# Exponentials left in PSUM, five PSUM banks given out by the list schedule, and late transposes moved to DMA, in an RWKV attention with a multiplicative FFN

## The chip, the cores and the metric

The kernel runs on one core of a Trainium2 chip. The metric is the device time of one launch in microseconds. Smaller is better.

## The reference

```python
B, H, S, D = 4, 8, 768, 48                       # r, k, v, w: [B, H, S, D], u: [H, D], all float32
state = zeros(B, H, D, D)
for t in range(S):
    kt, vt, rt, wt = k[:, :, t], v[:, :, t], r[:, :, t], w[:, :, t]
    cur = einsum('bhd,bhe->bhde', u * kt, vt)
    y[:, :, t] = einsum('bhd,bhde->bhe', rt, state + cur)
    state = wt[..., None] * state + einsum('bhd,bhe->bhde', kt, vt)

x = y.transpose(0, 2, 1, 3).reshape(B * S, H * D)     # 3072 tokens x 384
out = ((x @ w1) * (x @ w2)) @ w3 @ w_out              # 384 -> 1024 -> 1024 -> 384
```

## The kernel before

**Tiling.** The 3072 tokens are cut into 24 chunks of 128 tokens, six for each of the four sequences. A chunk holds all eight heads, so a row of a chunk is 8 x 48 = 384 numbers. The FFN works on blocks of two or four chunks (2, 2, 4, 4, 4, 4, 4).

**The attention of one chunk n**, with the names that its steps have in the code and in the profile:

- The loads `ld_w`, `ld_k`, `ld_r`, `ld_v` bring w, k, r and v of the chunk from DRAM, 192 KB each. SP issues them; there are eight buffers of each kind. k and r lie side by side in one tile, `kr_in`.
- `ln` (ACT) takes the logarithm of w. `cs` (PE, two matmuls) sums it over the tokens with triangular matrices. `ex` (ACT) takes the exponentials, which before go from PSUM to the tile `e_sb` in SBUF. `krt` (DVE) multiplies k and r by them and writes bf16.
- `tr` (PE, eight 128x128 transposes) and `trs` (ACT, copy from PSUM) turn the scaled k and r so that the head dimension lies on the partitions.
- `m` (PE) makes the scores, and `mb` (DVE, tile `mbf`) masks them. `kv` (PE) makes the chunk's contribution to the state and, in an extra column, the chunk's total decay in logarithm. `pc` (ACT) takes its exponential.
- `ts` (DVE) forms the running state, before with four fused multiply-adds; `sbd` (POOL) multiplies it by the decay into a block-diagonal bf16 tile, in two instructions.
- `uk1`, `uk2` (POOL, tile `uk`), `ds` (DVE) and `yd` (POOL) make the u term. `vb` turns v into bf16 (tile `v_bf`).
- `y` (PE) sums the masked scores times v and r times the state of the chunk before; `yb` (DVE, tile `y_bf`) adds the u term. `yt` (PE, three transposes) and `xt` (ACT) turn the result for the FFN, into `xT`.

**The FFN.** For each block and each of eight slices of 128 hidden columns, `a` and `b` (PE, three matmuls each) are formed, `a` is copied to SBUF by ACT (`a_sb`) and DVE multiplies the two (`abT`). w3 and w_out are multiplied once, on the chip: `wt`, `wtc`, `wm`, `wc` make `w34`. `o` (PE, eight matmuls for 128 tokens), a copy by ACT (`o_sb`) and a store issued by SP end it.

**The order of the work.** Nothing is executed in the order in which it is written down. Every step above is given to the class `Plan` with its engine, a planned length, the steps that it needs, the buffers that it takes and frees. `Plan` runs a list schedule: at each turn the step that can start first is placed, and of steps that can start at the same time the one with the lowest rank. The planned times of loads come from a model of the DMA ring with at most eight transfers in flight. The steps are then emitted in the order found, each engine works through its own list in that order, and semaphores enforce the data. So the order on every engine, SP's queue included, is fixed at build time by planned times, and a step that comes later than planned holds everything behind it on its engine. All instructions are emitted through one helper, so that nearly all of them carry one line number.

**The weights** are loaded by DMAs that POOL issues, and that turn float32 into bf16. Each of the seven pieces waits for a POOL step named in `TUNE["triggers"]`.

**PSUM** has eight banks. Before, three belong to the FFN (`f`), two to `tr`, `kv` and `yt` in turn, a pair to `cs` and `m`, and one to `y`.

Of the kernel before, what the change touches and what calls it, by code (L numbers as in the profile page):

```python
# [16 lines left out]
    early=2,  # L17
    triggers=["uk10", "uk21", "uk12", "uk22", "uk22", "uk13", "uk23"],
    lead=5, every=3.9,
    m_one=True, s_dve=False, v_act=2, nudge={},  # L20
# [3 lines left out]
class Plan:  # L24
# [6 lines left out]

    HOP = 0.06
# [7 lines left out]
    def add(self, name, eng, length, fn, needs=(), take=(), free=(), lag=0.03, rank=None, rows=0, big=0):  # L40
        assert name not in self.steps, name
        self.steps[name] = dict(eng=eng, length=length, fn=fn, needs=list(needs), take=list(take),
                                free=list(free), lag=lag,
                                rank=(rank if rank is not None else len(self.steps)) + TUNE["nudge"].get(name, 0),
                                rows=rows, big=big)

    def _pass(self, windows):
        end, eng_free, taken, owner, released = {}, {}, {}, {}, {}
        left = dict(self.steps)
# [12 lines left out]
        while left:  # L62
            best = {}
            for n in ready:
# [14 lines left out]
                if not ok:  # L79
                    continue  # L80
                if s["rows"] and len(ring) >= 8:
                    t = max(t, ring[-8])
                best.setdefault(s["eng"], []).append((t, s["rank"], n))
# [9 lines left out]
            start[n] = t  # L93
            eng_free[s["eng"]] = t + s["length"]
# [25 lines left out]
            for u in users.get(n, ()):  # L120
                waiting[u] -= 1
                if waiting[u] == 0:
                    ready.add(u)
        return order, new_windows, start, end

# [27 lines left out]
def kernel(  # L153
# [49 lines left out]
    ps_t = ctx.enter_context(tc.tile_pool(name="ps_t", bufs=2, space=bass.MemoryType.PSUM))  # L203
    ps_m = ctx.enter_context(tc.tile_pool(name="ps_m", bufs=1, space=bass.MemoryType.PSUM))
    ps_y = ctx.enter_context(tc.tile_pool(name="ps_y", bufs=1, space=bass.MemoryType.PSUM))
# [4 lines left out]
    mask = consts.tile([C, HP, C], BF)  # L210
# [16 lines left out]
                       base=0, channel_multiplier=-1, pattern=[[0, HP], [1, C]])  # L227
# [14 lines left out]
    for i in range(NS):  # L242
# [4 lines left out]
    plan.buffers(w_in=NIN, kr_in=NIN, v_in=NIN, lw=NS, krt=NS, sbd=NS, v_bf=3, e_sb=2, uk=2, ds=2, yd=3,  # L247
                 trs=2, mbf=2, pc=3, ts=3, y_bf=2, a_sb=3, o_sb=3, xT=3, abT=3, w3T=2, f=3, t=2, m=1, y=1)
    T = {}
    EV = -50  # L250
# [34 lines left out]
    def att(n):  # L285
        b, c = divmod(n, NC)
        last = c == NC - 1
        v_act = n >= TUNE["v_act"]
# [5 lines left out]
        def cs():  # L294
            t = T["cs", n] = ps_m.tile([C, 2, TB], F32, tag="m", name="cs")
            for j, lt in enumerate((LTn_incl, LT_strict)):
                pe.matmul(t[:, j, 0:DM], lhsT=lt, rhs=T["lw", n][:, :, 0:D], start=True, stop=True)

        def ex():
            t = T["e", n] = work.tile([C, 2, H, D], F32, tag="e_sb", name="e_sb")  # L300
            act.activation(t.rearrange("t j h d -> t j (h d)"), T["cs", n][:, :, 0:DM], Act.Exp)

        def krt():
            T["krt", n] = kr_st[n % NS]
            dve.tensor_mul(T["krt", n][:, :, :, 0:D], T["kr_in", n], T["e", n])
# [13 lines left out]
        def ds():  # L319
            t = T["ds", n] = work.tile([C, H], F32, tag="ds", name="ds")  # L320
            dve.reduce_sum(t, T["uk", n], axis=mybir.AxisListType.X)
# [5 lines left out]
        def tr():  # L327
            t = T["tr", n] = ps_t.tile([C, 2, HP, C], BF, tag="t", name="tr")
# [5 lines left out]
        def trs():  # L334
            t = T["trs", n] = work.tile([C, 2, HP, C], BF, tag="trs", name="trs")
            act.copy(t, T["tr", n])

        def kv():
            t = T["kv", n] = ps_t.tile([C, HP, D + 1], F32, tag="t", name="kv")
# [9 lines left out]
        def pc():  # L349
            t = T["pc", n] = work.tile([C, HP], F32, tag="pc", name="pc", bufs=3)  # L350
            act.activation(t[:, :, None], T["kv", n][:, :, D:D + 1], Act.Exp)

        def ts():
            t = T["ts", n] = work.tile([C, HP, D], F32, tag="ts", name="ts_", bufs=3)
            if c == 0:
                dve.tensor_copy(t, T["kv", n][:, :, 0:D])
            else:
                for p in range(HP):
                    dve.scalar_tensor_tensor(t[:, p, :], T["ts", n - 1][:, p, :], T["pc", n - 1][:, p:p + 1],
                                             T["kv", n][:, p, 0:D], op0=Alu.mult, op1=Alu.add)  # L360

        def sbd():
            t = T["sbd", n] = sb_st[(b * (NC - 1) + c) % NS]
            for q in range(2):
                o = q * DP
                (dve if TUNE["s_dve"] else pool).tensor_mul(
                    t[o:o + DP, :, q * D:(q + 1) * D], T["ts", n][o:o + DP],
                    T["pc", n][o:o + DP, :, None].to_broadcast([DP, HP, D]))

        def m():  # L370
            t = T["m", n] = ps_m.tile([C, 2, HP, C], F32, tag="m", name="m")
# [7 lines left out]
        def mb(q):  # L379
            if q == 0:  # L380
                T["mb", n] = work.tile([C, 2, HP, C], BF, tag="mbf", name="mbf")
            if TUNE["m_one"]:
                dve.tensor_mul(T["mb", n].rearrange("s q h t -> s (q h) t"),
                               T["m", n].rearrange("s q h t -> s (q h) t"),
                               mask[:, 0:1, :].to_broadcast([C, H, C]))
            else:
                dve.tensor_mul(T["mb", n][:, q], T["m", n][:, q], mask)

        def y():
            t = T["y", n] = ps_y.tile([C, H, D], F32, tag="y", name="y")  # L390
            first = True
            if c > 0:
                for p in range(HP):
                    pe.matmul(t[:, 2 * p:2 * p + 2, :], lhsT=T["trs", n][:, 1, p, :],
                              rhs=T["sbd", n - 1][:, p, :], start=first, stop=False)
# [7 lines left out]
        def yb():  # L403
            t = T["yb", n] = work.tile([C, DM], BF, tag="y_bf", name="y_bf")
            dve.tensor_add(t.rearrange("t (h e) -> t h e", h=H), T["y", n], T["yd", n])

        def yt():
            t = T["yt", n] = ps_t.tile([C, DI, C], BF, tag="t", name="yt")
# [6 lines left out]
        def xt():  # L415
            if n == lo:
                T["xT", j] = big.tile([P, DI, TB], BF, tag="xT", name="xT")
            act.copy(T["xT", j][:, :, (n - lo) * C:(n - lo + 1) * C], T["yt", n])

        A = plan.add  # L420
        A(f"ln{n}", "ACT", 0.46, ln, needs=[f"ld_w{n}"], take=["lw"], free=[f"ld_w{n}"])
        A(f"cs{n}", "PE", 0.33, cs, needs=[f"ln{n}"], take=["m"], lag=0.2, free=[] if not last else [f"ln{n}"])
        A(f"ex{n}", "ACT", 0.75, ex, needs=[f"cs{n}"], take=["e_sb"], free=[f"cs{n}"])
        A(f"krt{n}", "DVE", 1.12, krt, needs=[f"ex{n}", f"ld_k{n}", f"ld_r{n}"], take=["krt"],
          free=[f"ex{n}", f"ld_k{n}"])
        A(f"tr{n}", "PE", 0.46, tr, needs=[f"krt{n}"], take=["t"], lag=0.2, free=[] if not last else [f"krt{n}"])
        A(f"trs{n}", "ACT", 0.95, trs, needs=[f"tr{n}"], take=["trs"], free=[f"tr{n}"])
        A(f"vb{n}", *(("ACT", 0.43) if v_act else ("POOL", 0.55)), vb, needs=[f"ld_v{n}"], take=["v_bf"], free=[f"ld_v{n}"])
        if not last:
            A(f"kv{n}", "PE", 0.42, kv, needs=[f"krt{n}", f"vb{n}"], take=["t"], lag=0.2,  # L430
              free=[f"krt{n}", f"ln{n}"])
            old = [f"ts{n - 1}", f"pc{n - 1}"] if c else []
            A(f"ts{n}", "DVE", 0.48 if c else 0.32, ts, needs=[f"kv{n}"] + old, take=["ts"], free=[f"kv{n}"] + old)
            A(f"pc{n}", "ACT", 0.14, pc, needs=[f"kv{n}"], take=["pc"], free=[f"kv{n}"])
            A(f"sbd{n}", *(("DVE", 0.55) if TUNE["s_dve"] else ("POOL", 1.25)), sbd, needs=[f"ts{n}", f"pc{n}"],
              take=["sbd"], free=[f"ts{n}", f"pc{n}"])
        A(f"m{n}", "PE", 0.36, m, needs=[f"trs{n}"], take=["m"], lag=0.2)
        if TUNE["m_one"]:
            A(f"mb0{n}", "DVE", 1.17, lambda: mb(0), needs=[f"m{n}"], take=["mbf"], free=[f"m{n}"])
        else:  # L440
            A(f"mb0{n}", "DVE", 0.63, lambda: mb(0), needs=[f"m{n}"], take=["mbf"], free=[f"m{n}"])
            A(f"mb1{n}", "DVE", 0.63, lambda: mb(1), needs=[f"mb0{n}"], free=[f"m{n}"])
        A(f"uk1{n}", "POOL", 1.06, uk1, needs=[f"ld_k{n}", "ld_u"], take=["uk"])
        A(f"uk2{n}", "POOL", 1.06, uk2, needs=[f"uk1{n}", f"ld_r{n}"], free=[f"ld_k{n}"])
        A(f"ds{n}", "DVE", 0.5, ds, needs=[f"uk2{n}"], take=["ds"], free=[f"uk1{n}"])
        A(f"yd{n}", "POOL", 0.85, yd, needs=[f"ds{n}", f"vb{n}"], take=["yd"], free=[f"ds{n}"])
        A(f"y{n}", "PE", 0.42, y, needs=[f"mb0{n}" if TUNE["m_one"] else f"mb1{n}", f"vb{n}"] + ([f"sbd{n - 1}"] if c else []), take=["y"], lag=0.2,
          free=[f"mb0{n}", f"trs{n}", f"vb{n}"] + ([f"sbd{n - 1}"] if c else []))
        A(f"yb{n}", "DVE", 0.5, yb, needs=[f"y{n}", f"yd{n}"], take=["y_bf"], free=[f"y{n}", f"yd{n}"])
# [161 lines left out]
```

## Time and profile before

| | |
|---|---|
| median of 8 runs | 193.96 us (192.83 to 195.13) |
| the profiled execution | 195.13 us, of which the span is 193.4 us |
| TensorE clock granted | 1.0 |
| busy: PE, DVE, ACT, POOL | 166.2, 129.2, 116.9, 106.0 us |
| moved by DMA | 28.54 MB, mean 148 GB/s |

The profile is one execution. Its page gives busy time by engine, the span in 40 slices of 4.8 us with the busy share of each in tenths, the chain of work that ended last, and groups of instructions. A group's line reads: engine, operation, output and input tiles with partitions x elements, count, busy time and mean of one in ns, and the engine's idle time before them with what ended most of it. In a list of waits the numbers are the sum in us, how many, and the longest. In the list of instructions in order of time they are start, length, engine, operation, tiles and count; several alike are merged into one entry. PE's busy time counts the latency of pipelined matmuls, so it is more than what the matmuls need when they stream.

### The profile page before, as it was taken

Reading aid. Unit: us, or ns where it says so; the run is one execution under the profiler, and the core shown is the slowest. Engines: PE = TensorE matmul, PEld = TensorE weight load, DVE = VectorE, ACT = ScalarE, POOL = GpSimd, SP = SyncE. Lnnn points to the kernel's source line nnn. Section 1 sums busy time; section 2 is a strip of 40 time slices with the busy share of each in tenths; the row PEclk is TensorE's granted clock in tenths of the full one; section 3 lists DMA queues with packets and bytes.
Section 4 is the critical chain, followed back from the end, with each engine's and each line's share of the span. In section 5 each row is a group of like instructions: output and inputs, shape, how many; then the busy total and the mean of one; then the engine's idle time right before and its main releaser. Section 6 shows DMA issues by size and latency. Waiting matters only on the chain.

```text
span 193.4 us, 4437 instructions
## 1 busy us (share of the span) xinstructions
PE 166.2 (86%) x1658; PEld 103.7 (54%) x1672; DVE 129.2 (67%) x238; ACT 116.9 (60%) x227; POOL 106.0 (55%) x133
## 2 busy tenths in 40 slices
PE   0437896979999989999899999999699999999992
PEld 0214675856776655545565464666355664454450
DVE  6256768554697779897686999797688745422510
ACT  3426455631787777877867976975776834434431
POOL 5498897220496898977795968969623200000000
PEclk9999999999999999999999999999999999999999
DMA  6999999999799899999999989999200021013012
GB/s 117 200 178 171 204 215 190 203 201 185 131 190 191 169 226 195 224 159 192 189 169 235 220 180 187 161 198 218 103 2 3 37 90 41 0 41 124 3 52 111
DMA packets 107159, 28.54 MB, mean 148 GB/s; under 512 B 100353, under 2 KB 106113, under 8 KB 107137
## 3 DMA queue, kind: packets, MB, share of 16 engines
q1 hardware_dynamic: 103440, 23.80, 64.7%
q0 software_dynamic: 3696, 4.46, 13.6%
q8 instruction: 13, 0.21, 0.6%
q14 instruction: 10, 0.07, 0.1%
HBM read 27.98 MB, written 4.72 MB: 169 GB/s over the span
## 4 chain that ended last, share of the span: by engine, by line
PE 44%; DMA 17%; POOL 16%; DVE 8%; ACT 6%; issue 5%; SPq 2%; POOLq 0%; ACTq 0%; DVEq 0%
PE o_ps L148 11%; POOL uk L148 8%; PE b L148 7%; PE a L148 7%; DMA w_bf<-in_moe_w_dram 7%; DMA kr_in<-in_k_dram 6%; PE wm L148 6%; POOL sbd L148 4%; POOL yd L148 4%; ACT e_sb L148 3%; PE tr L148 3%; DVE krt L148 2%; DMA out_dram<-o_sb 2%; DVE mbf L148 2%; PE kv L148 2%
## 5 line engine op out<-in xcount | busy, mean ns | idle before, releaser
L148 PEld LDWEIGHTS <-w_bf 128*128 128x128 bf16 x400 | 35.4, 98 | 27.5 <-issue 2.2
L148 DVE TENSOR_TENSOR abT<-a_sb,b 128x512 bf16<-128x512 f32 (+1 forms) x56 | 33.9, 606 | 22.6 <-PE b L148 12.4
L148 PE MATMUL b<-xT,w_bf 128*128 128x512 bf16 (+1 forms) x161 | 39.9, 350 | 1.0 <-ACT a_sb L148 0.5
L148 PE MATMUL a<-xT,w_bf 128*128 128x512 bf16 (+1 forms) x161 | 39.6, 349 | 1.1 <-ACT xT L148 0.6
L148 ACT COPY a_sb<-a 128x512 f32<-128x512 f32 (+1 forms) x56 | 29.4, 528 | 17.7 <-PE a L148 15.6
L148 PE MATMUL o_ps<-w,abT 128*128 128x384 bf16 x192 | 34.2, 326 | 0.0
L148 POOL TENSOR_TENSOR yd<-v_bf,ds 128x384 bf16<-128x384 bf16 x24 | 25.3, 1054 | 12.8 <-ACT v_bf L148 9.9
L148 DVE TENSOR_TENSOR krt<-kr_in,e_sb 128x768 bf16<-128x768 f32 x24 | 25.6, 1068 | 10.0 <-ACT e_sb L148 9.9
L148 DVE TENSOR_TENSOR mbf<-m,mask 128x1024 bf16<-128x1024 f32 x24 | 29.1, 1214 | 1.5 <-PE m L148 1.5
L148 POOL TENSOR_TENSOR uk<-uk,kr_in 128x384 f32<-128x384 f32 x24 | 25.7, 1073 | 7.3 <-DMA kr_in<-in_r_dram 6.1
L148 POOL TENSOR_TENSOR uk<-kr_in,u_bc 128x384 f32<-128x384 f32 x24 | 25.5, 1064 | 7.6 <-DMA kr_in<-in_k_dram 4.7
L148 ACT COPY trs<-tr 128x1024 bf16<-128x1024 bf16 x24 | 24.4, 1016 | 5.7 <-PE tr L148 5.2
L148 PEld LDWEIGHTS <-krt 128*128 128x128 bf16 (+1 forms) x352 | 17.5, 109 | 15.1 <-DVE krt L148 8.1
L148 PEld LDWEIGHTS <-abT 128*128 128x128 bf16 x192 | 17.8, 98 | 11.6
L148 ACT ACTIVATE e_sb<-cs 128x768 f32<-128x768 f32 x24 | 19.6, 817 | 5.6 <-PE cs L148 5.5
L148 PE MATMUL tr<-I,krt 128*128 128x128 bf16 x192 | 16.0, 231 | 5.0 <-DVE krt L148 5.0
L148 ACT COPY o_sb<-o_ps 128x384 f32<-128x384 f32 x24 | 11.5, 478 | 14.5 <-PE o_ps L148 11.1
L148 ACT ACTIVATE lw<-w_in 128x384 bf16<-128x384 f32 x24 | 12.5, 526 | 7.0 <-DMA w_in<-in_w_dram 7.0
L148 DVE TENSOR_REDUCE ds<-uk 128x8 f32<-128x384 f32 x24 | 13.1, 545 | 5.3 <-POOL uk L148 4.8
L148 DVE TENSOR_TENSOR y_bf<-y,yd 128x384 bf16<-128x384 f32 x24 | 13.2, 550 | 4.5 <-issue 1.9
L148 PEld LDWEIGHTS <-trs 48*128 48x128 bf16 (+1 forms) x272 | 11.6, 99 | 8.3 <-issue 3.0
L148 PE MATMUL cs<-lw,LTn_incl 128*128 128x384 bf16 x24 | 8.4, 351 | 7.2 <-ACT lw L148 5.0
(80 smaller groups left out, 183.5 us busy)
## 6 DMA issues: line engine op xcount, KB each, us to landing
w_in<-in_w_dram SPq DMA_DIRECT2D x24, 192.0 KB, 4.6
kr_in<-in_k_dram SPq DMA_DIRECT2D x24, 192.0 KB, 4.6
kr_in<-in_r_dram SPq DMA_DIRECT2D x24, 192.0 KB, 4.7
v_in<-in_v_dram SPq DMA_DIRECT2D x24, 192.0 KB, 4.6
out_dram<-o_sb SPq DMA_DIRECT2D x24, 192.0 KB, 2.0
w_bf<-in_moe_w_dram POOLq DMA_DIRECT2D x2, 1024.0 KB, 15.5
w_bf<-in_moe_w_dram POOLq DMA_DIRECT2D x4, 384.0 KB, 6.7
wo_bf<-in_moe_w_out_dram POOLq DMA_DIRECT2D x1, 768.0 KB, 11.3
```

Of the source, the lines that this page charges most:

```text
L148: return self.tc.keep_in_program_order(f(*a, **k))
```

## The change

- `ex` writes the exponentials back over the sums in PSUM, and `krt` reads them there; the tile `e_sb` is gone. `pc` does the same with the decay column of `kv`.
- The five banks outside the FFN become three tiles, `g01`, `g23` and `g4`. `cs` and `m` take one of two pairs, and `tr`, `kv`, `y` and `yt` take one of five banks. `Plan` chooses at its turn the bank that comes free first by its planned times; the bank is held until the steps named in `free` are done.
- For chunks 12 to 23, `tr` is dropped and `trs` is a DMA that transposes the scaled k and r from SBUF to SBUF (128 x 1024, bf16). For chunks 16 to 23, `yt` is dropped and `xt` is such a DMA of 128 x 384. SP issues both.
- The state: `ts` adds the chunk's contribution to the decayed state, `st` multiplies by the decay (one DVE instruction each), and `sb` copies it into the block-diagonal tile (POOL, two instructions).
- The mask has one 128 x 128 block; `trs` and `y_bf` get three buffers; SP's steps of non-negative rank may be planned no earlier than 1.5 us before the modelled DMA ring is free.
- Planned lengths, ranks and settings change: which POOL step lets each weight piece go, how many FFN blocks come before `w34` in rank (`early`), and how far the attention's ranks run ahead (`lead`, `every`). `s_act`, `d_pool` at NEVER leave `sb` on POOL and `ds` on DVE.

```diff
 TUNE = dict(
     blocks=[2, 2, 4, 4, 4, 4, 4],
-    early=2,
-    triggers=["uk10", "uk21", "uk12", "uk22", "uk22", "uk13", "uk23"],
-    lead=5, every=3.9,
-    m_one=True, s_dve=False, v_act=2, nudge={},
+    early=1,
+    triggers=["uk11", "uk21", "uk21", "uk23", "uk23", "uk23", "uk23"],
+    lead=4, every=4.0,
+    v_act=2, s_act=NEVER, d_pool=NEVER, y_dma=16, kr_dma=12, ahead=1.5, nudge={},
 )
...
+    SLOTS = {1: [(4,), (0,), (1,), (2,), (3,)], 2: [(0, 1), (2, 3)]}
...
+                if s["bank"]:
+                    slot = self._slot(s["bank"], holder, freed, frees, released)
+                    if slot is None:
+                        continue
+                    t = max(t, slot[0])
                 if s["rows"] and len(ring) >= 8:
                     t = max(t, ring[-8])
+                if s["rows"] and s["rank"] >= 0:
+                    t = max(t, ring_free - TUNE["ahead"])
...
+    def _slot(self, size, holder, freed, frees, released):
+        best = None
+        for slot in self.SLOTS[size]:
+            held = [holder[i] for i in slot if i in holder]
+            if any(freed.get(o, 0) < frees[o] for o in held):
+                continue
+            t = max([0.0] + [released[o] + self.HOP for o in held])
+            other = 0 if size == 2 or slot[0] == 4 else 1
+            key = (t, other, slot)
+            if best is None or key < best:
+                best = key
+        return best
...
         def ex():
-            t = T["e", n] = work.tile([C, 2, H, D], F32, tag="e_sb", name="e_sb")
-            act.activation(t.rearrange("t j h d -> t j (h d)"), T["cs", n][:, :, 0:DM], Act.Exp)
+            t = T["cs", n][:, :, 0:DM]
+            act.activation(t, t, Act.Exp)
...
-            t = T["trs", n] = work.tile([C, 2, HP, C], BF, tag="trs", name="trs")
-            act.copy(t, T["tr", n])
+            t = T["trs", n] = work.tile([C, 2, HP, C], BF, tag="trs", name="trs", bufs=3)
+            if n < TUNE["kr_dma"]:
+                act.copy(t, T["tr", n])
+            else:
+                sp.dma_start_transpose(t.rearrange("d j p t -> d (j p) t"),
+                                       T["krt", n].rearrange("t j h d -> t (j h d)"))
...
-                for p in range(HP):
-                    dve.scalar_tensor_tensor(t[:, p, :], T["ts", n - 1][:, p, :], T["pc", n - 1][:, p:p + 1],
-                                             T["kv", n][:, p, 0:D], op0=Alu.mult, op1=Alu.add)
...
+                dve.tensor_add(t, T["st", n - 1], T["kv", n][:, :, 0:D])
+
+        def st():
+            t = T["st", n] = work.tile([C, HP, D], F32, tag="st", name="st_")
+            dve.tensor_mul(t, T["ts", n], T["kv", n][:, :, D:D + 1].to_broadcast([C, HP, D]))
...
-            act.copy(T["xT", j][:, :, (n - lo) * C:(n - lo + 1) * C], T["yt", n])
+            x = T["xT", j][:, :, (n - lo) * C:(n - lo + 1) * C]
+            if n < TUNE["y_dma"]:
+                act.copy(x, T["yt", n])
+            else:
+                sp.dma_start_transpose(x, T["yb", n])
...
+        if n < TUNE["kr_dma"]:
+            A(f"tr{n}", "PE", 0.46, tr, needs=[f"krt{n}"], bank=1, lag=0.2, free=[f"krt{n}"])
+            A(f"trs{n}", "ACT", 0.98, trs, needs=[f"tr{n}"], take=["trs"], free=[f"tr{n}"])
+        else:
+            A(f"trs{n}", "SP", 0.06, trs, needs=[f"krt{n}"], take=["trs"], free=[f"krt{n}"], rows=1500, rank=-3)
...
+            A(f"xt{n}", "SP", 0.06, xt, needs=[f"yb{n}"], take=["xT"] if n == lo else [], free=[f"yb{n}"], rows=560,
+              rank=-2)
```

## The prediction

> **What bounds the kernel now.** I read the page's shares and slices first, then the SP queue in order of time, then the chain that ended last.
>
> ```profile
> PE 166.2 (86%) x1658; PEld 103.7 (54%) x1672; DVE 129.2 (67%) x238; ACT 116.9 (60%) x227; POOL 106.0 (55%) x133
> ...
> PE   0437896979999989999899999999699999999992
> DVE  6256768554697779897686999797688745422510
> ACT  3426455631787777877867976975776834434431
> POOL 5498897220496898977795968969623200000000
> ...
> DMA  6999999999799899999999989999200021013012
> ```
>
> A slice is 193.4/40 = 4.8 us. DMA stands at 8 or 9 through slice 27, to about 135 us, and then falls to nothing; PE is full from about 45 us to the end. So there are two stages: one in which the loads are the scarce thing, and one in which PE works off what has piled up. The SP queue in order of time shows the first:
>
> ```profile
> 114.90 1.10 SPq L148 DMA_DIRECT2D w_in<-in_w_dram  x1
> 116.12 0.93 SPq L148 DMA_DIRECT2D kr_in<-in_k_dram  x1
> ...
> 130.16 0.99 SPq L148 DMA_DIRECT2D kr_in<-in_r_dram  x1
> 131.20 0.95 SPq L148 DMA_DIRECT2D v_in<-in_v_dram  x1
> 132.25 27.28 SPq L148 DMA_DIRECT2D out_dram<-o_sb  x8
> ```
>
> Between 114.90 and 132.25 SP issues 16 loads and nothing else: 17.35/16 = **1.08 us a load**, one issue directly after another. It isn't engines that hold it:
>
> ```profile
> SPq L148 <- ACT o_sb L148: 50.3, 13, 15.8
> SPq L148 <- ACT xT L148: 2.5, 5, 0.7
> ```
>
> The 50.3 us are stores, which wait for results, mostly after the last load. The loads are thus paced by the DMA engines. The page's issues say how late a load lands in a full ring and a store in a nearly empty one (last column):
>
> ```profile
> kr_in<-in_r_dram SPq DMA_DIRECT2D x24, 192.0 KB, 4.7
> ...
> out_dram<-o_sb SPq DMA_DIRECT2D x24, 192.0 KB, 2.0
> ```
>
> The second stage, from the chain (start, length, what):
>
> ```profile
> 158.62 0.37 PE y L148 x12
> ...
> 170.16 5.20 PE o_ps L148 x32
> ...
> 184.43 5.21 PE o_ps L148 x32
> 189.71 0.48 ACT o_sb L148
> ```
>
> The y at 158.62 is the last chunk's. From its end, 158.99, PE runs FFN back to back until 189.64: **30.6 us of backlog**. Then come the last copy and store: 193.4 - 189.64 = 3.76 us.
>
> The chain's other pieces give PE's price of a step when it streams: o_ps 1.30, a or b 0.65 (512 wide; 0.33 at 256), wm 1.30, wt and tr 0.45, kv 0.42, y 0.37, m 0.33, cs 0.33; yt is 3/8 of tr, 0.17. Times their counts (16 narrow and 40 wide of a and of b; o 24, wm and wt 8, kv 20, the rest 24): 62.6 + 31.2 + 10.4 + 3.6 + 10.8 + 8.4 + 8.9 + 7.9 + 7.9 + 4.1 = **155.8 us of PE work**. Up to 158.99 it has done 155.8 - 30.6 = 125.2, so 33.8 us were lost, some 12 of them in the first 20 us.
>
> **What the Trainium skill says.** (1) Advanced Engine Details and Errata, X-Bar Transpose (TRN2): transposing DMAs are as fast as plain ones. (2) DMA: Bandwidth & Descriptors, Latency and other measured facts: 261 GB/s for one such kernel. (3) VectorE: DVE Perf Modes, The three transpose paths: 1309 ns for one 128x128 block. No transposing DMA is in the trace of before, so nothing there agrees or disagrees. (4) SBUF — State Buffer, Who interferes with whom: a DVE instruction with two SBUF inputs and a GpSimd one that reads SBUF block each other. The trace agrees: krt takes 959 ns in the median, 1767 at most; uk 998 and 1594.
>
> **The change, part by part.**
>
> *Transposes to DMA.* Chunks 12 to 23 lose tr on PE and trs on ACT; chunks 16 to 23 lose yt and xT.
>
> ```profile
> L148 ACT COPY trs<-tr 128x1024 bf16<-128x1024 bf16 x24 | 24.4, 1016 | 5.7 <-PE tr L148 5.2
> ...
> L148 PE MATMUL tr<-I,krt 128*128 128x128 bf16 x192 | 16.0, 231 | 5.0 <-DVE krt L148 5.0
> ```
>
> PE: 12 x 0.45 + 8 x 0.17 = 6.8 us less, so 149.0. ACT: 12 x 1.02 + 8 x 0.48 = 16.1 us less, but ACT is 60% busy and only its short waits stand on the path. SP's queue gets 12 transposes of 256 KB and 8 of 96 KB. Price of a large one, T: by (1), 1.08 us, as a load; by (2), 262144 B / 261 GB/s = 1.0; by bytes against a load (256/192 x 1.08), 1.44; by (3), eight blocks that don't overlap, 10.5. I take the byte ratio, **T = 1.44**, and 3/8 of it, 0.54, for a small one. All of it is on the path: the DMA engines have nothing to hide it with before 135 us.
>
> *SP's order.* In the built program every transpose waits for its krt (or y_bf) on DVE, and the loads behind it in SP's queue wait too. Up to eight transfers are in flight, about 4.6 us of work, which cover such a wait; without that cover it costs its length. Ahead of the last r load stand 10 large and 5 small transposes, and 12 stores where before had 8 (a store at half a load, 0.5; at most 1.08). So that load is issued at 130.16 + 14.4 + 2.7 + 2.0 = 149.3.
>
> *From there to the end.* It lands 4.6 later, 153.9; krt 1.0, 154.9; its transpose stands behind the v load, another large and a small one, between the 2.0 of an empty ring and the 4.7 of a full one, I take 3.3: 158.2; m, mask product (1.21), y with hand-overs 2.2: **160.4**, against 158.99. After the last y the built order leaves PE three o_ps, 16 a or b and four o_ps: 3.9 + 10.4 + 5.2 = 19.5 us, where before has 30.6. The small transposes of the last two chunks (2 to 3 us) lie beside the three o_ps; without them they would be bare. 160.4 + 19.5 + 3.8 = **183.7 by DMA**. As a formula: 165.2 + 12.9 T.
>
> *The same by PE.* At 149.0 of work and before's loss of 33.8 up to the last y, PE reaches it at 129.5 + 33.8 = 163.3, and the end is 163.3 + 19.5 + 3.8 = **186.6**. The larger counts; since the other parts cut a few waits I take a span of 185.5.
>
> *Exponentials in PSUM, and krt from it.* Exp 812 ns, between equal and a tenth less; krt has one SBUF input, so (4) no longer applies: from its mean of 1068 towards 959, 24 x 0.11 = 2.6 us of DVE, and as much on POOL. The bank pair is held about 1 us longer, until krt has read it; before cs and m share one pair, now there are two. What is late next when this wait shrinks is the load.
>
> *State.* Four fused instructions (0.78 us a chunk) become one add and one product, each like the copy of the same size (0.35): 20 x 0.70 = 14.0 against 16 x 0.78 + 4 x 0.35 = 13.9, nothing. The block copy on POOL is a copy where it was a product (504 ns, twice): by the v cast of twice the width (505 at least) between 0.25 and 0.5, 0 to 10 us of POOL, which ends long before PE. It stands one DVE step later, hidden by the chunk until the next y reads it; if it were not, 20 x 0.4 = 8 us at most.
>
> *Banks.* tr, kv, y and yt choose among five banks by a planned time. Nothing in the trace shows this; between +3 (a bank held where the plan took it for free) and -6 (of the 33.8 lost, POOL's waits for pc and DVE's for e_sb are the cue). I take 0 beyond the above.
>
> *Weights, ranks, smaller mask.* The first piece goes out one chunk later, the third a little earlier, the fourth to sixth up to a chunk later. A 13.55 us wait on w_bf, ended at 42.0, stands in the chain; the same bytes come from the same queue, and FFN of the first two blocks still precedes wt. Zero, plus or minus 1.5.
>
> **To the median.** The profiled execution took 195.13 us: 1.73 beside its span, and 1.17 above the median of 193.96. 185.5 + 1.73 - 1.17 = **186.1**, I say 186.0. About 0.5% either way, 1 us, is what a measurement here can tell from no change.
>
> **The rivals.** *A, as above*: 182 to 190, chance 0.52. *B, transposes as cheap as loads and fewer waits*: T = 1.08 gives 179.1; PE then has to lose only 29, which lighter ACT, POOL and five banks must bring. For: 12 of the 33.8 lost can't go, 22 can. Against: POOL, DVE and PE are each at 9 tenths in places. 177 to 182, chance 0.26. *C, the cover fails*: SP waits for DVE with the ring run dry, 0.6 us at each of 12, and 185.5 becomes 193: no change, chance 0.05. *D, slower*: a transposing DMA that holds the engines for longer. 165.2 + 12.9 T reaches 193.4 at **T = 2.2**, twice a load; at 3 us it is 204. For: (3), and a saturated queue with nothing to absorb it. Against: (1) and (2). Chance 0.17. *E, the transposes aren't what helps*: PE and ACT didn't pace the second half, and an earlier FFN order does it all; this gives A's time, and the backlog after the last y would show it.
>
> **How the numbers follow.** 186.0 is A's. The range, 178.5 to 195.5, takes A, C, most of B, and D up to T = 2.3. Faster by over 0.5%: A and B, 0.78; within: 0.05; slower: 0.17.
>
> **What would show it.** After: DMA at 9 to about 155 us instead of 135; the last r load issued near 149; last y near 160 to 163; 19.5 us of PE work behind it; trs landing in 3 to 5 us; krt near 960 ns with no long ones; SP waits on DVE of a few us. Wrong, if the transposes land in over 8 us, if the last y is before 152, or if PE's backlog after it isn't near 20.

## The result, and the profile after

The changed kernel takes **191.07 us** (median of 11 runs, 189.79 to 195.54) against 194.12 us (median of 32 runs of before on the same chip): ratio **0.984 [0.981, 0.987]**. It is faster by 1.6%, where the prediction said 4%. The profiled execution took 189.79 us with a span of 188.1 us. It is the lowest of its 11, 1.28 us under their median, while the profiled execution of before lay 1.0 us above its own. So the two spans differ by 2.7% and the medians by 1.6%: some of what the two profiles show is scatter between executions.

From the page of after: busy times, slices (4.7 us each) and the hardware DMA queue (packets, MB, share of 16 engines' span).

```profile
PE 162.3 (86%) x1539; PEld 96.1 (51%) x1552; DVE 126.0 (67%) x210; ACT 103.9 (55%) x207; POOL 89.0 (47%) x133
...
PE   0466598599899999899999969999996999989992
...
DVE  6266547586367777798989977869784398904510
ACT  3335537546346887888776556656563456234431
POOL 4397595630237678576667246643347227100000
...
DMA  6999999999999999999998999998997999251013
...
q1 hardware_dynamic: 119440, 27.73, 78.2%
```

After the first slice DMA now stands at 8 or 9, once at 7, through slice 33 (counted from 0), to about 160 us, where before it fell away at 135. ACT and POOL have become lighter. PE has a 6 in slices 23 and 30 (108 to 113 and 141 to 146 us); the chain below has a transfer that ends in each. The packets of the hardware queue took 0.782 x 188.1 us of the 16 engines, 22.0 us more than the 64.7% of 193.4 us on the page of before. That is for 12 large and 8 small transposes, 15 large ones by bytes: 1.46 us each. But e7 below moves the same packets, and there they took 85.6% of 185.9 us, 12 us more than here. So this difference gives no price to rely on.

SP's queue in order of time (start, length of the issue, tiles), up to the last loads:

```profile
144.09 0.53 SPq L179 DMA_DIRECT2D kr_in<-in_k_dram  x1
144.72 0.53 SPq L179 DMA_DIRECT2D out_dram<-o_sb  x1
145.34 1.29 SPq L179 DMA_TRANSPOSE trs<-krt  x1
146.72 0.53 SPq L179 DMA_DIRECT2D out_dram<-o_sb  x1
147.30 0.43 SPq L179 DMA_DIRECT2D kr_in<-in_r_dram  x1
147.83 0.65 SPq L179 DMA_DIRECT2D out_dram<-o_sb  x1
148.53 0.42 SPq L179 DMA_DIRECT2D v_in<-in_v_dram  x1
149.61 0.33 SPq L179 DMA_DIRECT2D out_dram<-o_sb  x1
149.99 0.43 SPq L179 DMA_DIRECT2D w_in<-in_w_dram  x1
150.73 1.32 SPq L179 DMA_TRANSPOSE xT<-y_bf  x1
152.15 0.53 SPq L179 DMA_DIRECT2D kr_in<-in_k_dram  x1
152.73 0.57 SPq L179 DMA_DIRECT2D kr_in<-in_r_dram  x1
```

The last r load goes out at **152.73**, predicted 149.3. SP is issuing nearly all the time (between the r loads of chunks 15 and 23 its issues sum to 53.0 of 59.8 us), but in another way than before. There, a load's issue lasted about as long as the load's turn in the DMA engines (0.93 to 1.10 us). In the lines above a load or store takes 0.33 to 0.65 us, and a transpose 1.3, whether it is large (`trs`) or has three eighths of the bytes (`xT`). Between those two r loads a large one held SP for 1.24 to 3.03 us, 1.84 in the mean, and a small one for 1.28 in the mean. The last two small ones took nearly as long, though the first of them was issued with no other DMA of SP's under way:

```profile
164.26 1.18 SPq L179 DMA_TRANSPOSE xT<-y_bf  x1
165.53 0.53 SPq L179 DMA_DIRECT2D out_dram<-o_sb  x1
166.16 1.18 SPq L179 DMA_TRANSPOSE xT<-y_bf  x1
```

Next to it, the landing times of the transposes (median), what SP waits for, and the products that fed them:

```profile
trs<-krt SPq DMA_TRANSPOSE x12, 4.0
xT<-y_bf SPq DMA_TRANSPOSE x8, 2.9
```

```profile
SPq L179 <- ACT o_sb L179: 19.5, 9, 12.0
SPq L179 <- DVE y_bf L179: 9.1, 3, 5.4
SPq L179 <- DVE krt L179: 4.5, 3, 1.9
```

```profile
L179 DVE TENSOR_TENSOR krt<-kr_in,g 128x768 bf16<-128x768 f32 x24 | 22.7, 948 | 4.0 <-ACT g L179 3.4
L179 ACT COPY trs<-g 128x1024 bf16<-128x1024 bf16 x12 | 12.2, 1013 | 9.8 <-PE g L179 7.2
```

From the chain that ended last, two transfers on it and its end (`y_bf` follows the last y):

```profile
106.10 5.22 DMA trs<-krt
...
137.74 5.19 DMA v_in<-in_v_dram
...
161.74 0.87 PE g L179 x20
162.61 1.30 PE o_ps L179 x8
164.38 0.57 DVE y_bf L179
...
166.16 2.32 DMA xT<-y_bf
...
180.33 4.25 PE o_ps L179 x25
184.65 0.48 ACT o_sb L179
```

The last y is done at 164.3, and from there PE has 20.3 us to its end at 184.58; 3.5 us for copy and store follow.

### The profile page after: what moved, and what is told of

Read it like the earlier page. It is cut to its first block, busy times and chain, and to the rows that moved or that the text cites. A ratio compares the mean times of both kernels' runs of the same rounds, so it can differ in the third digit from the quotient of the medians.

```text
span 188.1 us, 4196 instructions
## 1 busy us (share of the span) xinstructions
PE 162.3 (86%) x1539; PEld 96.1 (51%) x1552; DVE 126.0 (67%) x210; ACT 103.9 (55%) x207; POOL 89.0 (47%) x133
## 4 chain that ended last, share of the span: by engine, by line
PE 70%; DVE 9%; DMA 8%; ACT 5%; issue 4%; SPq 2%; DVEq 0%; ACTq 0%
PE g L179 21%; PE b L179 15%; PE a L179 15%; PE o_ps L179 13%; PE wm L179 4%; DMA trs<-krt 3%; DMA v_in<-in_v_dram 3%; ACT trs L179 3%; DVE krt L179 3%; DVE mbf L179 2%; DMA w_in<-in_w_dram 2%; SPq L179 2%; PE wt L179 1%; ACT g L179 1%; DMA xT<-y_bf 1%
## 5 line engine op out<-in xcount | busy, mean ns | idle before, releaser
L179 ACT COPY a_sb<-a 128x512 f32<-128x512 f32 (+1 forms) x56 | 29.4, 525 | 23.6 <-PE a L179 22.6
L179 DVE TENSOR_TENSOR mbf<-g,mask 128x1024 bf16<-128x1024 f32 x24 | 29.3, 1221 | 6.7 <-PE g L179 6.7
L179 POOL TENSOR_TENSOR yd<-v_bf,ds 128x384 bf16<-128x384 bf16 x24 | 19.9, 830 | 21.1 <-DVE ds L179 14.2
L179 ACT ACTIVATE g<-g 128x768 f32<-128x768 f32 (+1 forms) x44 | 22.3, 508 | 13.4 <-PE g L179 9.7
L179 DVE TENSOR_TENSOR krt<-kr_in,g 128x768 bf16<-128x768 f32 x24 | 22.7, 948 | 4.0 <-ACT g L179 3.4
L179 PEld LDWEIGHTS <-trs 48*128 48x128 bf16 (+1 forms) x272 | 11.7, 100 | 16.1 <-ACT trs L179 4.5
L179 PEld LDWEIGHTS <-krt 128*64 128x64 bf16 (+1 forms) x256 | 11.3, 113 | 14.3 <-DVE krt L179 8.7
L179 DVE TENSOR_TENSOR y_bf<-g,yd 128x384 bf16<-128x384 f32 x24 | 13.3, 553 | 7.8 <-PE g L179 6.4
L179 ACT COPY trs<-g 128x1024 bf16<-128x1024 bf16 x12 | 12.2, 1013 | 9.8 <-PE g L179 7.2
L179 PE MATMUL g<-trs 48*128 48x128 bf16 x192 | 10.4, 233 | 4.7 <-ACT trs L179 2.2
L179 ACT CAST v_bf<-v_in 128x384 bf16<-128x384 f32 x22 | 11.3, 512 | 5.1 <-DMA v_in<-in_v_dram 3.2
L179 PE MATMUL g<-I,krt 128*128 128x128 bf16 x96 | 8.6, 242 | 5.7 <-DVE krt L179 5.6
## 6 DMA issues: line engine op xcount, KB each, us to landing
w_bf<-in_moe_w_dram POOLq DMA_DIRECT2D x2, 1024.0 KB, 19.1
wo_bf<-in_moe_w_out_dram POOLq DMA_DIRECT2D x1, 768.0 KB, 11.1
```

The costliest lines, as they stand in the source:

```text
L179: return self.tc.keep_in_program_order(f(*a, **k))
```

## The experiments

All ratios are against the kernel before on the same chip; its median there was between 192.26 and 194.65 us, so compare ratios and not medians. "Last r" is the issue of chunk 23's r load in the profiled execution. Most edits go through `Plan`, which then orders all engines anew; the edits of e4, e5, e10, e14, e15, e16 and e17 leave after's planned order as it is, and that of e18 leaves e2's. Those comparisons are the cleaner ones. A sliver is a DMA of 32 bytes a row (64 in e15) that stands for a whole transfer.

| kernel | median us | ratio [95%] | last r, us |
|---|---|---|---|
| before | 194.12 | 1 | 130.16 |
| after | 191.07 | 0.984 [0.981, 0.987] | 152.73 |
| e1 no transposes by DMA | 194.28 | 1.009 [1.006, 1.012] | 132.19 |
| e2 only k, r by DMA | 187.13 | 0.970 [0.964, 0.976] | 144.64 |
| e3 only y by DMA | 192.27 | 0.996 [0.993, 0.998] | 133.69 |
| e4 slivers in place of transposes | 188.85 | 0.981 [0.976, 0.987] | 151.21 |
| e10 the same, tiles filled by POOL | 185.01 | 0.959 [0.952, 0.966] | 147.29 |
| e5 each transpose twice | 212.67 | 1.103 [1.096, 1.109] | 173.2 |
| e6 settings of before | 192.88 | 0.997 [0.994, 1.001] | 154.2 |
| e7 stores late | 186.69 | 0.969 [0.964, 0.975] | 146.42 |
| e8 exponentials in SBUF | 193.90 | 1.004 [1.001, 1.007] | 153.46 |
| e9 settings of before, no transposes by DMA | 195.12 | 1.012 [1.004, 1.020] | 131.7 |
| e11 before, stores late | 190.27 | 0.986 [0.979, 0.993] | 124.07 |
| e12 stores late, y by DMA from chunk 8 | 189.94 | 0.984 [0.978, 0.991] | 152.5 |
| e13 only k, r by DMA, stores late | 186.94 | 0.961 [0.954, 0.968] | 138.10 |
| e14 slivers in place of y transposes | 187.44 | 0.960 [0.953, 0.968] | 149.31 |
| e15 slivers in place of 16 stores | 190.08 | 0.974 [0.966, 0.982] | 153.25 |
| e16 stores issued by ACT | 202.97 | 1.055 [1.051, 1.060] | 165.22 |
| e17 20 DMAs of 32 bytes more | 199.65 | 1.036 [1.033, 1.040] | 160.00 |
| e18 e2 with stores issued by ACT | 202.52 | 1.052 [1.048, 1.056] | 158.17 |

**The transposes as a whole (e1, e4, e10, e5).**

```diff
 # e1
-    y_dma=16, kr_dma=12
+    y_dma=NEVER, kr_dma=NEVER
```

> The changed kernel with all transposes back on PE and ACT; list schedule planned anew. It has the banks, the exponentials in PSUM, the state's new form and the new settings. Theory 1: loads end near 132 as before the change, and PE with 155.8 us of work, some 33 lost and 3.5 after it ends near 192: the DMA transposes are then worth only the 1 to 4 us by which the changed kernel is faster than this, since they take 6.8 us from PE and add 22 to the DMA engines. Theory 2: PE's and ACT's relief is all there is, this kernel is at 194 to 196, like before. A third outcome, faster than the changed kernel (under 190): moving the transposes costs more than it brings, and the gain is the PSUM part's.

Slower than before by 0.9%, and 2.5% slower than after: it is the transposes by DMA that gain, and the rest of the change costs a little without them. Some of that cost goes with the granted clock: the three of e1's executions that had a mean clock of 1.0 took 193.0 to 193.3 us, about 0.4% more than before. Rival E falls.

```diff
 # e4 and e10, in trs and xt; the tiles are static, filled once by DVE (e4) or POOL (e10)
-    sp.dma_start_transpose(...)
+    t = trs_st[n % 3];  sp.dma_start(t[:, 0, 0, 0:16], krt[:, 0, 0, 0:16])
+    x = xT_st[j % 2];   sp.dma_start(x[:, 0, 0:16], y_bf[:, 0:16])
```

> Left out: the transposing DMAs of chunks 12 to 23 (scaled k and r) and 16 to 23 (y). In the place of each, at the same place in SP's queue and with the same waits, stands a DMA of 128 x 32 bytes into a static tile, which m, y and a, b then read. All engines keep their order. If the DMA engines pace the second half (theory 1), some 20 us of DMA work go: the last r load is issued near 132 to 135 us instead of 152.7, and the end comes earlier until PE bounds it: 149.0 us of work, 30 to 34 lost and 3.5 after it, a span of 179 to 186. If PE and the other engines pace it and the transposes are hidden (theory 2), the span stays at 187 to 190 although the loads come earlier. If the transposes' latency is what costs (theory 3), little changes, as the small DMAs keep some 2 us each.

> Left out, as in the first kernel of this kind, is the work of the 20 transposing DMAs: slivers of 128 x 32 bytes at the same places with the same waits. The static tiles are now filled by POOL while it waits for v near 45 us, since the first time their filling on DVE held PE back by about 2.7 us between 40 and 60 us. If the DMA work costs the changed kernel some 4 us (what PE gained after 60 us in the first try), the span comes to 183 to 185. If it costs nothing, 187 to 189.

e4's filling by DVE held PE back between 40 and 60 us (16.4 us busy of 20, where after has 19.2), so it tells nothing. e10, in the planned order of after, gains 2.5% on it, 4.9 us, though all of the transposes' DMA work is gone. The last r load comes only 5.4 us earlier, since SP then waits for something else:

```profile
SPq L179 <- DVE krt L179: 9.1, 6, 2.6
```

That is e10's list of SP's waits between 60 and 153 us; in the same stretch after has 2.6 us of it, in two waits. PE was at 19.7 to 19.8 us busy of 20 from 80 to 140 us. So with next to no work in the transposes, PE and the wait for krt bind.

```diff
 # e5, behind each of the 20 transposes
+    sp.dma_start_transpose(scr, same source)
```

> Each of the 20 transposing DMAs is issued twice in a row, the second time into a tile that nobody reads. Order otherwise unchanged. Theory 1 (DMA paces): the last r load moves later by 10 large and 5 small transposes, at 1.44 and 0.54 us that is 17 us, and the end by as much or a little more (two more large ones ahead of the last y): span 203 to 209. Theory 2 (transposes hidden beside engine work): 188 to 192. In between would give the share of a transpose that is on the path.

1.103 against 0.984 is 23 us more than after, with the last r load 20.5 us later for 10 large and 5 small transposes more. Downward the path yields 4.9 us, upward it costs everything: after seems to sit at the knee where SP's queue and PE both bind.

**Which transposes (e2, e3, e14).**

```diff
 # e2: y_dma=NEVER, kr_dma=12      e3: y_dma=16, kr_dma=NEVER
 # e14, in xt alone; the static tiles are filled once by POOL
-    sp.dma_start_transpose(x, T["yb", n])
+    x = xT_st[j % 2];  sp.dma_start(x[:, 0, 0:16], T["yb", n][:, 0:16])
```

> The changed kernel with only k and r of chunks 12 to 23 transposed by DMA, y on PE and ACT; planned anew. The 20 transposes together bring 2.5% (1.009 without them, 0.984 with). By their relief of PE, the large ones are 5.4 of 6.8 us, so four fifths of it if relief counts: 0.99. If the small ones cost more than they bring, since they are late in the chain (y_bf, DMA, a), this is faster than the changed kernel.

> Only y of chunks 16 to 23 transposed by DMA. By relief a fifth of 2.5%: 1.00 to 1.005. If the two kinds need each other to take ACT and PE out of the late attention, nothing: 1.009.

> Left out: the transposes of y of chunks 16 to 23; a DMA of 128 x 32 bytes with the same waits stands at each place and a, b read a static tile. Order as in the changed kernel. If their ring work makes the changed kernel slower than the one with k and r alone, the last r load comes 2.7 us earlier or more and the span falls to 185 to 186.5. If it is the order (SP waiting for y_bf with loads behind it, 9.1 us in three waits), no change: 187 to 189.

k and r alone give 3.0%, y alone 0.4%, both together 1.6%. The y transposes cost more than they bring: without them (e2) the kernel is 1.4% faster than after, and with their work taken away in the unchanged order (e14) 2.4%. The prediction counted them as the cheap ones. From e14's chain; its last y ends just ahead of the second line, at 160.9:

```profile
159.27 1.30 PE o_ps L179 x8
...
160.94 3.90 PE o_ps L179 x24
```

**The stores (e7, e11, e12, e13, e15).** In the order of after 16 stores stand ahead of the last r load, in that of before 8.

```diff
 # e7 (from after), e11 (from before): stores wait until the last xT is made
-    needs=[f"os{j}.{t_}"]            o_sb=3
+    needs=[f"os{j}.{t_}", f"xt{NU - 1}"]   o_sb=20
 # e12: e7 with y_dma=8       e13: e7 with y_dma=NEVER
 # e15, for the first 16 stores
-    sp.dma_start(out3[lo + t_], T["os", j, t_])
+    sp.dma_start(out3[lo + t_][:, 0:16], T["os", j, t_][:, 0:16])
```

> All 24 stores are held back in SP's queue until the last transpose of y, with 20 buffers for o_sb; planned anew. Of the changed kernel's stores 16 stand ahead of the last r load, at 0.5 to 1.1 us each in the DMA ring. Theory 1: 8 to 12 us of DMA work leave the paced stretch, the last r load is issued near 143 and the span falls by 4 to 8, to 180 to 184, unless the stores then hold the end (24 x 0.6 = 14 us, which fit beside the last 20 us of PE). Theory 2: no change, 187 to 190.

> The kernel before with all its stores held back until the last copy of y, with 20 o_sb buffers, planned anew. In the changed kernel this cut 1.5%. If DMA already paced the kernel before (what the prediction built on), 8 stores of 0.5 us leave its loads and 2 to 4 us come off: 0.98 to 0.99. If PE and its losses pace it, as its 30.6 us of backlog behind the last y say, nothing: 0.995 to 1.005.

> Late stores, and y transposed by DMA from chunk 8 instead of 16: 8 x 0.54 = 4.3 us more for the DMA engines, 1.4 less for PE, 3.9 less for ACT. If the late stores left room in the ring, a little faster than with late stores alone (0.9694): 0.96 to 0.97. If DMA still binds, slower: 0.975 to 0.99.

> k and r alone transposed by DMA, and all stores late; planned anew. The DMA side would let the last r load go near 138. Then PE binds: 150.4 us of work with 31 to 34 lost and 3.5 after it, span 185 to 187, ratio 0.96 to 0.97, no better than either change alone. If the two gains add, 0.955.

> Left out: of the first 16 stores all but 16 of 384 columns, so 64 of 1536 bytes a row. The order on every engine is the changed kernel's. If the stores' ring work is the mis-sized term (0.76 us each, from the 6.1 us by which the last r load of the kernel before came earlier without its 8), the last r load comes 6 to 11 us earlier, limited by how early the transposes ahead of it are ready, and the end 3 to 5 us: span 183 to 185.5. If a store costs its place and its wait rather than its bytes, no change: 187 to 190.

Late stores gain 1.4% before and 1.5% after. Both orders are planned anew, so this alone is no proof, but it fits a kernel before that SP's queue paced as well. For before, this edit brings nearly as much (0.986) as the whole change (0.984). From this I first took a store to cost 0.76 us of DMA work (6.1 us for 8). e15 contradicts that: with 23 of 24 bytes of these stores gone, in the same order, the last r load is where it was (153.25). e15's ratio is 1.0% lower than after's, which the two intervals hardly separate. Two stores of e15 from SP's queue, each for 8 KB where after moves 192:

```profile
145.34 0.53 SPq L179 DMA_DIRECT2D out_dram<-o_sb  x1
...
147.29 0.63 SPq L179 DMA_DIRECT2D out_dram<-o_sb  x1
```

They hold SP as long as the full ones: 0.68 us in the mean of the 12 between the r loads of chunks 15 and 23, where after's take 0.66. e12 says the same from the other side: 16 stores fewer and 8 small transposes more ahead of the last r load leave it at 152.5, so these nearly cancel, though a small one moves half the bytes of a store.

**DMA engines' work or SP's time (e16, e17, e18).**

```diff
 # e16 (from after) and e18 (from e2), stores of the first five blocks
-    sp.dma_start(out3[lo + t_], T["os", j, t_])
+    (act if j < 5 else sp).dma_start(out3[lo + t_], T["os", j, t_])
 # e17, behind each of the 20 transposes
+    sp.dma_start(fill[0:1, i:i + 16], mask[0:1, 0:16])
```

> The changed kernel with one more DMA behind each of its 20 transposes, of 32 bytes in one row: a queue's issue with next to no work for the DMA engines; 15 of them stand ahead of the last r load. Theory R: last r load at 152 to 154, ratio 0.982 to 0.99. Theory S: 15 x 0.6 = 9 us later, at 160 to 162, and 1.02 to 1.035 in all. In between, by the share of the stretch in which SP has no slack.

> The first 16 stores are issued from ACT's queue at the same places of the planned order; all else stays in the changed kernel's order. Theory R, the DMA engines' work paces the loads: the bytes are the same, so the last r load stays at 152 to 153.5 and the ratio near 0.984 (0.979 to 0.989). Theory S, SP's own time to issue paces them (0.53 us for each store, 0.1 between instructions, plus the waits of the stores for o_sb that hold the loads behind): 16 x 0.63 = 10 us less of SP's time, the last r load at 143 to 147, and the ratio 0.965 to 0.972, as where the stores were late, since PE binds next.

> k, r alone transposed by DMA (the y transposes on PE and ACT), with the first 16 stores issued from ACT's queue. Theory R: as k, r alone, 0.967 to 0.973, last r load at 144 to 145. Theory S: the last r load at 136 to 140; PE, which has 8 transposes more to do, binds before that is all gained: 0.955 to 0.965.

e17 decides: 20 DMAs of 32 bytes cost **about 10 us** (199.65 against 0.984 x 192.26 = 189.2), and the last r load is issued 7.3 us later for the 15 ahead of it, 0.48 each. In its queue they look like this, with the last r load below:

```profile
124.53 1.39 SPq L179 DMA_TRANSPOSE xT<-y_bf  x1
125.97 0.58 SPq L179 DMA_DIRECT2D fill<-mask  x1
126.65 0.53 SPq L179 DMA_DIRECT2D out_dram<-o_sb  x1
...
160.00 0.56 SPq L179 DMA_DIRECT2D kr_in<-in_r_dram  x1
```

Another reading would be that a DMA of any size takes one of the eight places in flight that `Plan` reckons with. The traces rule it out: by their issues and landings, at most five of SP's DMAs were under way whenever it issued one between the r loads of chunks 15 and 23, in every kernel of the table above.

e16 and e18 don't separate the two readings. ACT's queue stood for 11 us at its first store:

```profile
69.50 0.48 ACT L179 COPY xT<-g 128x384 bf16<-128x384 bf16 x1
80.53 0.37 ACTq L179 DMA_DIRECT2D out_dram<-o_sb  x1
81.00 1.01 ACT L179 COPY trs<-g 128x1024 bf16<-128x1024 bf16 x1 [11.01 <-DMA kr_in<-in_r_dram]
```

In the built program DMAs wait on eight completion semaphores, which SP's and ACT's seem to take in turn in the planned order. If so, the store waited for an r load that SP, behind its plan, had issued late; nothing behind it on ACT could run. PE ran dry; later SP stood from 91.5 to 107.9 us ahead of the first transpose, and the DMA engines were busy for 0.15 of that time. These runs say nothing on the stores' price.

**One account for all.** Between the issues of chunk 15's and chunk 23's r loads SP issues 32 loads and, by kernel, other numbers of the rest. A least-squares fit of five prices to 14 kernels, one profiled execution each, without e16 and e18:

| kernel | large | small | stores | slivers, fills | measured us | fit less measured |
|---|---|---|---|---|---|---|
| before | 0 | 0 | 4 | 0 | 37.0 | -0.2 |
| e11 | 0 | 0 | 0 | 0 | 35.0 | 0.0 |
| e1 | 0 | 0 | 8 | 0 | 39.0 | -0.4 |
| e3 | 0 | 2 | 8 | 0 | 41.0 | -0.3 |
| e13 | 9 | 0 | 0 | 0 | 47.6 | 0.1 |
| e2 | 10 | 0 | 9 | 0 | 51.9 | 1.2 |
| e8 | 8 | 5 | 12 | 0 | 56.1 | 0.7 |
| e12 | 9 | 9 | 0 | 0 | 56.1 | 1.0 |
| e7 | 11 | 4 | 0 | 0 | 56.3 | -1.6 |
| e14 | 10 | 0 | 12 | 5 | 56.6 | 0.1 |
| e15 | 10 | 5 | 0 | 12 | 59.3 | 0.5 |
| after | 10 | 5 | 12 | 0 | 59.8 | -0.1 |
| e17 | 10 | 5 | 12 | 15 | 67.0 | -0.5 |
| e5 | 20 | 10 | 12 | 0 | 79.5 | -0.5 |

Load **1.09**, large transpose **1.41**, small transpose **1.05**, store **0.44**, a DMA with next to no bytes **0.46**. e6 and e9, not in the fit, come out at 60.0 and 37.5 and measured 60.6 and 38.5. e4 and e10 don't fit (e10: 47.1 and measured 54.1); they are the ones in which SP waits 9 us and more for krt. The fit's own standard error is 0.06 for a large one, 0.09 for a small one and 0.05 for a store. A store costs what an empty DMA costs, and a small transpose about three quarters of a large one. A fit that ties the small one to 3/8 of the large one is 3.0 us off for e2; one that makes both equal (1.28) is nowhere off by more than 2.0. So stores and small transposes don't go by their bytes, and e15 and e17 put that on SP's time for each issue. What share of a large one's 1.41 is the engines' work and what SP's issue stays open.

**The other parts (e6, e8, e9).**

```diff
 # e6: early=2, lead=5, every=3.9 and triggers as before
 # e9: e6 with y_dma=NEVER, kr_dma=NEVER
 # e8: ex writes to a tile e_sb in SBUF (two buffers), krt reads that
```

> The changed kernel with early, triggers, lead and every as before the change. If these four settings are what makes the version without DMA transposes slower than before (PE busy 15.98 of 20 us between 20 and 40, where before has 17.55), this is 1 to 3 us faster than the changed kernel, 188 to 190. If they suit the new plan, it is 1 to 4 us slower.

> No DMA transposes and the settings of before, so only the PSUM part remains: exponentials in PSUM, five banks given out by the plan, the state in two steps, the copy on POOL, the smaller mask. If the PSUM part cuts waits, as the prediction had it, 188 to 191. If it is worth nothing, 192 to 193. If it is itself what costs, 194 to 196, as with the new settings.

> The changed kernel with the exponentials written to e_sb in SBUF again and krt reading them there, cs's pair free after ex; planned anew. Expected by the contention reading: krt back from 948 to about 1068 ns in the mean, long ones up to 1.7 us again, uk and yd on POOL longer too; as DVE is not what PE waits for most of the time, 0 to 2 us slower than the changed kernel. If the shorter hold of the bank pair matters more, faster by up to 2 us.

Under the settings of before the rest of the change (exponentials in PSUM, banks, state, mask), which e9 doesn't take apart, loses at the start and wins later. e9's windows (length, then busy time of PE, PEld, DVE, ACT, POOL, clock, DMA share, GB/s):

```profile
20.00:40.00 20.00, 11.71 (x115) 8.86 (x114) 9.16 (x17) 7.17 (x15) 7.29 (x10) 0.95 1.20 199
60.00:80.00 20.00, 20.00 (x249) 14.17 (x247) 16.98 (x30) 16.17 (x35) 15.55 (x21) 1.00 0.94 170
```

PE is busy for 11.7 us of the 20 to 40 stretch where before had 17.55 and after has 15.74, and for 20.0 of the 60 to 80 one, before 18.48. The new settings keep part of the second and repair part of the first: with the transposes they are worth 1.3% (e6 against after), without them 0.2%, which the intervals don't separate. e8 shows the exponentials in PSUM to be worth 2%, an order planned anew included; in it krt takes up to 1755 ns again and POOL is busy for 97.7 us instead of 89.0.

**The fastest that computes all** is e13, 186.94 us, 3.9% under before; e2 and e7 have 3.0 and 3.1%. Their two gains over after would add up to 0.955; e13's 0.961 [0.954, 0.968] can't be told from that. In e13 the last r load goes out at 138.1, 46.6 us before the end of the span of 184.7, where after has 35.4, and PE is busy for 79.3 us of the 80 to 160 stretch: there PE is what is left.

## Why the prediction missed

The direction was right, and so was rival A's course: SP's queue, with the transposes in it, sets when the last r load goes, and PE's FFN behind it sets the end. What the prediction had wrong is the price of what stands in that queue: it took DMA work by bytes, and nothing for SP's time to issue. 186.0 was 5.1 us too low, and the measured time lies in the range.

- **Transposes to DMA: the failed step is the small one.** For a large one the number was right, T = 1.44 against 1.41 in the fit, which excludes the 1.08 of rival B and the 2.2 of rival D. The reason given for it, work by bytes, isn't shown, so the agreement may be luck. "3/8 of it, 0.54, for a small one" was the byte ratio carried down, and a small one costs 1.05 on the path: 5 x 0.51 = 2.6 us. The trace of before has no transposing DMA, and up to its last load its queue held little but loads of one size, so that price by bytes and price by issue looked alike. The prediction gave bounds for T, but none for the small one, and took no price for SP's issue.
- **SP's order: the stores' price was near, their number wrong.** "12 stores where before had 8" should have been 16; at 0.44 that is 3.5 us instead of 2.0. The 0.5 was half a load, and e15 shows that a store's bytes don't make its price, so that hit is luck in part. "Up to eight transfers" in flight as cover was more than the at most five of the traces. With both terms the sum is 10 x 1.41 + 5 x 1.05 + 8 x 0.44 = 22.9 us, measured 152.73 - 130.16 = 22.6, predicted 19.1.
- **From there to the end: right in sum.** From the last r load to the last y 11.1 us predicted and 11.6 measured, PE's work behind it 19.5 and 20.3, the end 3.8 and 3.5. "183.7 by DMA" plus 3.4 at the load and 1.0 here is the measured 188.1.
- **The same by PE, and the choice of 185.5: wrong.** The 186.6 rested on PE's loss up to the last y being what it was, 33.8 us. It isn't a bound: e14, with the same PE work, ends its last y at 160.9 and has 19.7 us behind it, a loss of 31.6 (160.9 - (149.0 - 19.7)). In after the loss is 35.6 (164.3 - (149.0 - 20.3)); e14 differs only in SP's queue and in what a and b wait for, so most of these 4 us come from there. Having called the larger of two numbers the one that counts, the prediction went 1.1 us below it for "a few waits" that it did not name, which the loss of 35.6 doesn't bear out.
- **Exponentials, state.** krt lies at 942 to 955 ns with no long ones, as said. It was priced as 2.6 us of DVE with the load late next; e8, planned anew, puts it at 2% of the time, more than that. The block copies on POOL, 342 ns, lie in the range given.
- **Banks, weights and ranks.** Zero was not their size one by one: the PSUM part under the old settings is 1.2% slower (e9), and the new settings are worth 1.3% beside the transposes (e6). Together, without the transposes, they cost 0.9% (e1), which lies within the ends named, and on the side that the forecast did not lean to.
- **To the median.** The span was 2.6 us too low. The rest of the 5.1 is the conversion: the profiled execution of before lay 1.17 above its median, which was subtracted, and that of after 1.28 below its own. A part of after's median goes with the granted clock: its three executions at a mean clock of 0.999 or 1.0 took 190.1 to 191.2 us, the five at 0.982 190.8 to 191.8.
- **The signs named ahead.** DMA at 9 to 155: 160. The last r load near 149: 152.7. The last y near 160 to 163: 164.3, just outside. PE work behind it of 19.5: 20.3. trs landing in 3 to 5: 3.1 to 5.3. SP's waits on krt a few us: 4.5. Rival C's failing cover isn't it.

## What to carry to other kernels

Price a DMA that joins a busy queue twice, by the DMA engines' work and by the issuing engine's time, and count all that the new order puts ahead of the late load, stores too. Here a small transfer was not cheap in proportion to its bytes: moving the large transposes and leaving the small ones where they were gave more than moving both, and so did stores that went behind the last load. Where two limits are close, a loss carried over from the old profile is no bound, and no gain without a name belongs into the sum.

## What the runs showed of the hardware

- A transposing DMA from SBUF to SBUF held SP's queue for 1.2 us at least, at 128 x 384 as at 128 x 1024, where a plain one held it for 0.33 us at least and, in after's busy stretch, for 0.57 in the median. The large ones landed in 3.1 to 5.3 us. The Trainium skill's 1309 ns for one 128x128 block (VectorE: DVE Perf Modes, The three transpose paths) does not add up over eight blocks: eight in one DMA cost 1.41 us on the path. Its statement that transposing DMAs are as fast as plain ones (Advanced Engine Details and Errata, X-Bar Transpose (TRN2)) agrees with the fitted price of the large ones by bytes (1.41 us for 256 KB, a load's 1.09 for 192 KB), but not with that of the small ones (1.05 for 96 KB).
- A DMA of 32 bytes in one row held SP for about 0.6 us and delayed the later loads by 0.48 us each (e17).
- The granted TensorE clock dipped in most executions of the changed kernel and its relatives. In the profiled ones it did so for one or a few slices, as here in e1 from 34 to 43 us:

```profile
PEclk9999999589999999999999999999999999999999
```

  In e1 executions with a mean clock of 1.0 took 193.0 to 193.3 us, those at 0.982 193.7 to 194.6. What sets the dip off was not tried.
